# Strassen-form products for the first matmul of two MLPs, with operands streamed from DRAM and a planned instruction order

## Chip, cores and metric

The kernel runs on one core of one Trainium2 chip. The metric is device time in microseconds (us) of one execution; lower is better. The kernel before took 759.74 us (median of three runs, 759.37 to 760.29).

## What is computed

The input is q, k, v for 4 sequences of 576 tokens and 8 heads of 64. Attention is causal with a window of 128 and a linear bias by distance. Its output, 2304 tokens of 512 channels, goes through a first MLP (layer norm, 512 to 2048, relu, 2048 to 512, residual) and a second one (512 to 1024, relu, a gate made of a three-tap convolution along the sequence and a sigmoid, 1024 to 512):

```python
xn = (x - mu) / np.sqrt(var + 1e-06) * g_ln
x = x + np.maximum(xn @ w_ch1, 0.0) @ w_ch2
h = np.maximum(x @ w_in, 0.0)
conv_out += conv_w[k] * hp[:, k:k + S, :]          # k = 0, 1, 2
out = h * (1 / (1 + np.exp(-conv_out))) @ w_out
```

Weights arrive as 64-bit floats and are turned into 32-bit ones on the chip by integer operations on VectorE.

## The kernel before

The work is a pipeline on TensorE (PE) with three stages. Attention runs first (lines 333 to 737). The first MLP (lines 740 to 806) takes the 2304 tokens in six groups of 384 and, for each of 16 blocks of 128 hidden channels, calls `hidden` (line 314, first product) and `project` (line 759, second product). The second MLP (lines 809 to 963) takes the four sequences one by one: `hidden2` (line 869) makes one block of 128 hidden channels for 576 tokens, `gate_step` (line 884) runs relu, convolution, sigmoid and the split of the gated value, and `store` (line 819) makes the second product for 128 tokens and writes it out.

Every product is made three times: each operand is split into a high part (rounded, type fp32r, written by ScalarE) and a low part (the rest, written by VectorE), and high x high, high x low and low x high are summed in PSUM (`PASSES`, line 108). `split` (line 235) is the helper. So one block of `hidden` is 4 x 3 = 12 matmuls of 384 columns, one of `project` too, one of `hidden2` is 24 matmuls of 288 columns, and one `store` is 24 matmuls of 512 columns.

The order is written by hand. All engines issue in program order. In the first MLP, `hidden` of the next block stands ahead of `project` of the one before, so PE has 12 matmuls to do while ScalarE and VectorE split the hidden values. The layer norm of the next group is placed by tables of half steps (`LN_NEXT`, line 95), weight loads and conversions by `weights_step` (line 188), stores by `STORE_AT` (line 99). All weights of the first MLP stay in SBUF as high and low parts; those of the second are loaded in group 5 (lines 801 to 805) over them. Transfers are issued on SyncE's queue (SP).

Of the kernel before, what the change touches and what calls it, by code (L numbers as in the profile page):

```python
# [18 lines left out]
BIG = 2.0**110  # L19


@with_exitstack
def tile_kernel(
# [55 lines left out]
    NE = 7  # L79

# [9 lines left out]
    LN_SAME = {"spread2": {0: 1}}  # L90
    LN_FIRST = {
        "turn": {0: 6, 1: 9, 2: 11}, "root": {0: 13, 1: 14}, "gather": {0: 23}, "spread": {0: 25},
        "minus": {0: 27, 1: 28, 2: 29, 3: 30}, "parts": {0: 28, 1: 29, 2: 30, 3: 31},
    }
    LN_NEXT = {
        "turn": {0: 6, 1: 8, 2: 10}, "root": {0: 12, 1: 12}, "gather": {0: 14}, "spread": {0: 17},
        "minus": {0: 21, 1: 23, 2: 25, 3: 27}, "parts": {0: 22, 1: 24, 2: 26, 3: 28},
    }
    STORE_AT = {2: (0,), 3: ("mixed",), 4: (1,), 7: (2, 3)}
    SKIP = (4, 8, 12, 16, 20)  # L100
    LAST_CUTS = (256,)
    CONV_ACT = (0, 3, 5, 7)
    GATE_DVE = (0, 4, 6)
    VIA_PSUM = {"w1": 7, "w2": 9}
    SKIP_LAST = range(4, 31, 3)
# [9 lines left out]
    x = cpool.tile([P, NTT, DM], F32, tag="x", name="x")  # L115
    xT = x.rearrange("p t (c n) -> p t c n", n=P)

    pools = {"wearly": ctx.enter_context(tc.tile_pool(name="wearly", bufs=2 * NE))}
# [4 lines left out]
    c2pool.tile([P, 72], F32, tag="pad", name="pad")  # L123
# [5 lines left out]
    cvpool = xctx.enter_context(tc.tile_pool(name="cvpool", bufs=3, side="right"))  # L129
    dpool = xctx.enter_context(  # L130
        tc.tile_pool(name="dpool", bufs=2, space=bass.MemoryType.DRAM)
# [3 lines left out]
    fpool = xctx.enter_context(tc.tile_pool(name="fpool", bufs=2, side="right"))  # L135


    wtiles = {}
# [38 lines left out]
    def begin_loads(nm: str):  # L177
        scratch["raw"] = xnpool.tile([P, 3, 1024], I32, tag="xn_hl", name=f"raw_{nm}")
        scratch["n"] = 0
# [5 lines left out]
    COARSE = ((), ("rescale", 0, 1, 2), ("high", "low"))  # L185
    LAST = ((), ("rescale", 0, 1, 2), ("high",), ("low",))

    def weights_step(stages, start=True, only=None):
# [3 lines left out]
        for j in range(max((len(do) for _, do in now), default=0)):  # L192
            for ld, do in now:
                if j >= len(do):
                    continue
                kind, i, raw = ld["kind"], ld["i"], ld["raw"]
                if do[j] == "rescale":
                    t = ld["t"] = cvpool.tile([P, 512], I32, tag="cv", name=f"cv_{kind}_{i}")
                    if ld["via"]:
                        t = ld["mid"] = ps_x.tile([P, 512], I32, tag="px", name=f"cp_{kind}_{i}")  # L200
                    rescale(t, raw, G if stages is FINE else S)
                elif do[j] == "high":
                    w = wtiles[kind, i] = pools[ld["pool"]].tile(
                        [P, 2, 512], F32R, tag="w", name=f"{kind}_{i}"
                    )
                    S.activation(w[:, 0, :], ld["t"].bitcast(F32), AF.Copy)  # L206
                elif do[j] == "low":
                    w = wtiles[kind, i]
                    (G if stages is COARSE else V).tensor_tensor(  # L209
                        out=w[:, 1, :], in0=ld["t"].bitcast(F32), in1=w[:, 0, :].bitcast(F32),  # L210
                        op=ALU.subtract,
                    )
                    flight.remove(ld)
                else:
                    to_f32(ld["t"], raw, (do[j],), ld["mid"])
        if todo and start:
# [9 lines left out]
            else:  # L226
# [5 lines left out]
                "via": stages is COARSE and i >= VIA_PSUM[kind],  # L232
# [26 lines left out]
    def layer_norm(g: int, j: int, stage: str, pspool=None, tag=None):  # L259

        t = g * GT + j
        if stage == "turn":
            px = pspool.tile([P, NCC, P], F32, tag=tag, name=f"px_{t}")
            for c in range(NCC):
                T.transpose(px[:, c, :], xT[:, t, c, :], ident)
# [19 lines left out]
        elif stage == "gather":  # L285
# [5 lines left out]
            rows[g] = dpool.tile([2 * GT, P], F32, tag="rows", name=f"rows_{g}")  # L291
            nc.sync.dma_start(rows[g], mvt)
        elif stage in ("spread", "spread2"):

            i = stage == "spread2"
            b = bcs[g, i] = xnpool.tile([P, GT, P], F32, tag=f"bc{i:d}", name=f"bc{i:d}_{g}", bufs=1)
# [3 lines left out]
        elif stage == "minus":  # L300
            y = ys[g, j] = pools.get("y", fpool).tile([P, GT, P], F32, tag="y", name=f"xm_{g}_{j}")
            G.tensor_tensor(  # L302
                out=y, in0=xT[:, g * GT : (g + 1) * GT, j, :], in1=bcs[g, 0], op=ALU.subtract
            )
        else:
            if j == 0:
                xns[g] = xnpool.tile([P, 2, NCC, GN], F32R, tag="xn_hl", name=f"xn_hl_{g}")
# [6 lines left out]
    def hidden(g: int, f: int, pspool, tag: str):  # L314
        w = wtiles["w1", f]
# [9 lines left out]
        hh = hhs[g, f] = fpool.tile([P, 2, GN], F32R, tag="hh", name=f"hh_{g}_{f}")  # L325
# [7 lines left out]
    with ExitStack() as actx:  # L333
# [80 lines left out]
        reli = x[:, NTT - 3, 0:P].bitcast(I32)  # L414
# [11 lines left out]
        b0 = x[:, NTT - 4, 0:W]  # L426
        rows_i = x[:, NTT - 5, 0:NR].bitcast(I32)
        e = x[:, NTT - 5, 8 : 8 + NR]
        cb = x[:, NTT - 5, 16:20]
        sl = x[:, NTT - 5, 32 : 32 + NPAIR]  # L430
        ci = x[:, NTT - 6, 0:W].bitcast(I32)
        cf = x[:, NTT - 7, 0:W]
# [180 lines left out]
        def outputs(n: int):  # L613
# [3 lines left out]
            for u0, u1 in ((0, cut), (cut, 4)):  # L617
                if u0 < u1:
                    bl, pr, t = seq[n + u0]
                    t += bl * TPB  # L620
                    S.activation(xT[:, t : t + u1 - u0, pr, :], po[:, u0:u1], AF.Copy)
# [6 lines left out]
        for f in range(NF1):  # L628
            pool = "wearly" if f < NE else "wkeep" if f < NF2 else "wlate"
            todo += [("w1", f, pool), ("w2", f, pool)]  # L630
# [110 lines left out]
    pools["wkeep"] = ctx.enter_context(tc.tile_pool(name="wkeep", bufs=2 * NF2 - 2 * NE))  # L741
    ps_c = ctx.enter_context(tc.tile_pool(name="ps_c", bufs=1, space=PSUM, reuse_waits="tile"))
    with ExitStack() as fctx:
        pools["wlate"] = fctx.enter_context(tc.tile_pool(name="wlate", bufs=2 * (NF1 - NF2), reuse_waits="tile"))
        ps_h, ps_x = (
            fctx.enter_context(tc.tile_pool(name=n, bufs=2, space=PSUM, reuse_waits="tile"))
            for n in ("ps_h", "ps_x")
        )

        pcs = {}  # L750

        def residual(g: int, c: int, eng=G):
            xs = xT[:, g * GT : (g + 1) * GT, c, :]
            y = fpool.tile([P, GT, P], F32, tag="y", name=f"y_{g}_{c}")
            pc = pcs[g][c][:, :GN].rearrange("p (t n) -> p t n", n=P)
            V.tensor_tensor(out=y, in0=pc, in1=bcs[g, 1], op=ALU.mult)  # L756
            eng.tensor_tensor(out=xs, in0=y, in1=xs, op=ALU.add)  # L757

        def project(g: int, f: int):
            w, hh = wtiles["w2", f], hhs.pop((g, f))  # L760
            if f == 0:
                pcs[g] = [
                    ps_c.tile([P, 512], F32, tag=f"pc{c}", name=f"pc_{g}_{c}") for c in range(NCC)
                ]
            for c in range(NCC):
                pc = pcs[g][c]
                for n, (a, b) in enumerate(PASSES):
                    T.matmul(  # L768
                        pc[:, :GN], w[:, a, c * P : (c + 1) * P], hh[:, b, :],
                        start=f == 0 and n == 0, stop=f == NF1 - 1 and n == 2,  # L770
                    )
                if f == NF1 - 1 and g < NGRP - 1:
                    residual(g, c)

        steps = [(g, f) for g in range(NGRP) for f in range(NF1)]
        last = None
        for g, f in steps:
            for part in range(2):
                hs = 2 * f + part
                due = [(g, LN_SAME)]  # L780
                if g + 1 < NGRP:
                    due.append((g + 1, LN_NEXT if g else LN_FIRST))
                due = [
                    (gg, j, stage) for gg, table in due for stage, at in table.items()
                    for j in at if at[j] == hs
                ]
                for args in due:
                    if args[2] == "turn":
                        layer_norm(*args, ps_x, "px")
                if part == 0:  # L790
                    if (g, f) not in hhs:
                        hidden(g, f, ps_h, "ph")
                elif last is not None:
                    project(*last)
                for args in due:
                    if args[2] != "turn":
                        layer_norm(*args, ps_x, "px")
                if g == 0 or g == NGRP - 1:
                    weights_step(LAST if g else COARSE, 2 * f + part not in (SKIP if g == 0 else SKIP_LAST))
            last = (g, f)  # L800
            if g == NGRP - 1 and f == 0:
                begin_loads("win")
                for i in range(2 * NF2):
                    pool = "wearly" if i < 2 * NE else "wkeep"
                    todo.append(("win" if i < NF2 else "wout", i % NF2, pool))
        project(*last)


    bpool2, xpool = (
        ctx.enter_context(tc.tile_pool(name=n, bufs=b, reuse_waits="tile"))  # L810
        for n, b in (("bpool2", 2), ("xpool", 1))
    )
# [180 lines left out]
```

## Time and profile before

| what | us |
|---|---|
| runs: median (lowest to highest) | 759.74 (759.37 to 760.29) |
| profiled execution: span, first to last instruction | 757.7 |
| profiled execution: PE busy | 737.9 (97%) |
| PE weight load busy | 692.8 (91%) |
| VectorE (DVE) busy | 407.7 (54%) |
| ScalarE (ACT) busy | 314.7 (42%) |
| GpSimd (POOL) busy | 192.1 (25%) |

The profile gives the profiled execution's span, not its whole time; the median of the runs is 2.0 us above that span. To read it: one execution is shown; busy times are unions of the instructions of an engine. Matmuls are pipelined, so the mean of a single one (337 ns for 384 columns) is longer than the pitch at which they follow each other, and the pitch is read from chains of many. A share over the whole span mixes three stages with different limits.

### The profile page before, as it was taken

What the parts mean: (1) busy time and instruction counts of PE and PEld (TensorE: products, weight loads), DVE (VectorE), ACT (ScalarE), POOL (GpSimd) and SP (SyncE); (2) the same over time, 40 slices, a digit from 0 to 9 for tenths busy, and PEclk for the clock granted to TensorE, in tenths of its full rate; (3) what the DMA queues carried; (4) which work ended last, traced back from release to release, by engine and by line L of the source; (5) the groups of instructions that cost most, each with busy time, mean ns of one, the idle gap of its engine ahead of it and who ended that gap; (6) DMA issues with size and microseconds to landing.
All of it is one profiled execution on the core that took longest, in us unless ns stands there. A gap on an engine that the chain in (4) does not pass through costs nothing.

```text
span 757.7 us, 12569 instructions
## 1 busy us (share of the span) xinstructions
PE 737.9 (97%) x4896; PEld 692.8 (91%) x4896; DVE 407.7 (54%) x782; ACT 314.7 (42%) x840; POOL 192.1 (25%) x291
## 2 busy tenths in 40 slices
PE   7999998899999999999999999999999999999998
PEld 6777776799999999999999999999999889889987
DVE  6899999598732222122212312288789655456620
ACT  4888887545511111121112112154457554456521
POOL 1788789445620111112010221200023000000000
PEclk9999999999999999999999999999999999999999
DMA  6877765156300000000000000165100000000011
GB/s 149 186 188 164 190 164 133 33 187 176 113 12 8 4 1 11 11 1 10 1 12 1 12 12 1 25 208 179 44 1 1 28 15 29 29 28 15 15 42 56
DMA packets 81959, 47.25 MB, mean 62 GB/s; under 512 B 59440, under 2 KB 76652, under 8 KB 81900
## 3 DMA queue, kind: packets, MB, share of 16 engines
q1 hardware_dynamic: 80844, 46.20, 22.3%
q8 instruction: 38, 0.62, 0.4%
q10 hardware_dynamic: 1056, 0.26, 0.2%
q14 instruction: 21, 0.17, 0.1%
HBM read 41.71 MB, written 4.74 MB: 61 GB/s over the span
## 4 chain that ended last, share of the span: by engine, by line
PE 82%; DVE 11%; POOL 3%; ACT 2%; issue 1%; POOLq 0%; DVEq 0%; ACTq 0%
PE pc L768 25%; PE ph L320 25%; PE py L829 13%; PE pu L876 11%; PE ps L533 2%; DVE ps L544 2%; DVE pp L570 1%; PE po L608 1%; POOL pt L592 1%; DVE mn L548 1%; POOL pp L570 1%; DVE cv_w L172 1%; DVE cv_w L167 1%; PE ptp L580 1%; ACT pp L558 1%
## 5 line engine op out<-in xcount | busy, mean ns | idle before, releaser
L320 PE MATMUL ph<-xn_hl,w 128*128 128x384 f32 x1152 | 216.7, 337 | 0.0
L768 PE MATMUL pc<-hh,w 128*128 128x384 f32 x1152 | 215.7, 337 | 0.0
L768 PEld LDWEIGHTS pc<-hh,w 128*128 128x128 f32 x1152 | 200.6, 188 | 0.5 <-issue 0.2
L320 PEld LDWEIGHTS ph<-xn_hl,w 128*128 128x128 f32 x1152 | 200.2, 188 | 0.3 <-issue 0.2
L327 DVE SCALAR_TENSOR_TENSOR hh<-ph,hh 128x384 fp32r<-128x384 f32 x96 | 53.4, 556 | 205.8 <-ACT hh L326 205.6
L326 ACT ACTIVATE hh<-ph 128x384 fp32r<-128x384 f32 x96 | 47.1, 491 | 264.0 <-PE ph L320 263.9
L876 PEld LDWEIGHTS pu<-x,win 128*128 128x128 f32 x768 | 103.5, 188 | 1.6 <-ACT hp L889 0.6
L876 PE MATMUL pu<-x,win 128*128 128x288 f32 x768 | 104.5, 296 | 0.3 <-ACT hp L889 0.3
L829 PE MATMUL py<-wout,gm 128*128 128x512 f32 (+1 forms) x408 | 91.5, 382 | 0.0
L829 PEld LDWEIGHTS py<-wout,gm 128*128 128x128 f32 x408 | 73.0, 188 | 15.8
L902 DVE SCALAR_TENSOR_TENSOR cvo<-hp,cw,cvo 128x576 f32<-128x576 f32 x64 | 56.0, 875 | 3.7 <-POOL cvo L897 1.5
L558 ACT ACTIVATE pp<-ps,mn 128x128 f32<-128x128 f32 x144 | 51.3, 383 | 13.1 <-DVE mn L548 9.6
L302 POOL TENSOR_TENSOR xm<-x,bc 128x384 f32<-128x384 f32 x24 | 24.3, 1022 | 107.7 <-DVE xn_hl L244 57.9
L570 POOL TENSOR_SCALAR pp<-pp,sm 128x128 f32<-128x128 f32 x72 | 42.8, 604 | 33.1 <-DVE sm L567 30.5
L592 POOL TENSOR_SCALAR_AFFINE_SELECT pt<-pc 128x512 f32<-128x512 f32 x72 | 47.2, 684 | 1.7 <-ACT pc L585 1.4
L533 PE MATMUL ps<-kt,qt 64*128 64x256 f32 x288 | 44.0, 400 | 2.5 <-ACT pp L558 1.7
L608 PE MATMUL po<-pt,rawv 128*64 128x128 f32 x544 | 37.7, 280 | 7.8 <-POOL pt L592 5.6
L608 PEld LDWEIGHTS po<-pt,rawv 128*64 128x64 f32 x544 | 28.9, 136 | 16.2 <-POOL pt L592 13.3
L835 ACT ACTIVATE o<-py 128x512 f32<-128x512 f32 (+1 forms) x19 | 10.9, 575 | 64.3 <-PE py L829 64.3
L757 POOL TENSOR_TENSOR x<-y,x 128x384 f32<-128x384 f32 x20 | 19.6, 1015 | 66.3 <-DVE y L756 66.3
L239 DVE TENSOR_TENSOR gm<-cvo,gm 128x512 fp32r<-128x512 f32 x32 | 22.5, 703 | 23.7 <-ACT gm L238 23.6
L209 POOL TENSOR_TENSOR w<-cv_w,w 128x512 fp32r<-128x512 f32 x20 | 26.2, 1310 | 33.2 <-ACT w L206 31.9
(109 smaller groups left out, 812.3 us busy)
## 6 DMA issues: line engine op xcount, KB each, us to landing
raw_w<-in_moe_w_ch SPq DMA_DIRECT2D x32, 512.0 KB, 3.7
out<-o SPq DMA_DIRECT2D x17, 256.0 KB, 2.0
rawq<-in_q SPq DMA_DIRECT2D x32, 128.0 KB, 3.7
rawv<-in_v SPq DMA_DIRECT2D x32, 128.0 KB, 2.8
raw_win<-in_moe_w_in SPq DMA_DIRECT2D x8, 512.0 KB, 5.0
raw_win<-in_moe_w_out SPq DMA_DIRECT2D x8, 512.0 KB, 3.4
rawk<-in_k SPq DMA_DIRECT2D x30, 128.0 KB, 3.3
bc<-rows SPq DMA_DIRECT2D x12, 192.0 KB, 3.1
```

The lines of the kernel that those rows point to most:

```text
L320: T.matmul(ph[:, :GN], w[:, a, c * P : (c + 1) * P], xns[g][:, b, c, :], start=n == 0, stop=n == 3 * NCC - 1,)
L326: S.activation(hh[:, 0, :], ph[:, :GN], AF.Relu)
L327: V.scalar_tensor_tensor(out=hh[:, 1, :], in0=ph[:, :GN], scalar=0.0, in1=hh[:, 0, :].bitcast(F32), op0=ALU.max, op1=ALU.subtract,)
L533: T.matmul(ps[:, h, u, :].rearrange("p (o j) -> p o j", o=2), lhs, rhs, start=i == 0, stop=i == 1,)
L558: S.activation(pp[:, u, h, :], sc[:, h, u], AF.Exp, bias=mn[:, h, u : u + 1], scale=-1.0, accum_out=sm[:, 0, i : i + 1],)
L570: (G if i % 2 else V).tensor_scalar(out=pp[:, i, :], in0=pp[:, i, :], scalar1=sm[:, 1, i : i + 1], scalar2=1.0, op0=ALU.mult, op1=ALU.mult,)
L592: G.affine_select(out=parts[:, i], in_=pc, compare_op=ALU.is_ge, fill=0.0, base=base, pattern=[[0, 4], [sign, P]], channel_multiplier=-sign,)
L608: T.matmul(po[h * D : (h + 1) * D, u, :], rvs[bl, pr][:, t - 1 + i, h, :], pt[:, i, 2 * u + h, :], start=i == i0, stop=i == 1,)
L768: T.matmul(pc[:, :GN], w[:, a, c * P : (c + 1) * P], hh[:, b, :], start=f == 0 and n == 0, stop=f == NF1 - 1 and n == 2,)
L829: T.matmul(py[:, :w], lhs(a, f), wtiles["wout", f][:, b, c0:c1], start=n == 0, stop=n == 3 * NF2 - 1,)
L876: T.matmul(pu[:, i, :HS], w[:, a, c * P : (c + 1) * P], x2[:, i2, c, i * HS : (i + 1) * HS], start=n == 0, stop=n == 3 * NCC - 1,)
L902: V.scalar_tensor_tensor(out=cv, in0=hp[:, j : j + SEQ], scalar=cw[:, j * NF2 + f : j * NF2 + f + 1], in1=cv, op0=ALU.mult, op1=ALU.add,)
```

## The change

Only the two first products change arithmetically. Two blocks of tokens, two blocks of input channels and two blocks of hidden channels form 2 x 2 block matrices, whose product is made of 7 block products instead of 8, by sums of blocks of both operands. In the first MLP groups 0 and 1 stay as they were; groups (2, 3) and (4, 5) are the pairs, for 8 pairs of hidden blocks each (`superquad`). In the second MLP the two halves of each sequence are the pair, for 4 pairs of hidden blocks each (`quad2`). Each block product is 6 matmuls (2 channel blocks x 3 passes).

Operands. The seven token operands of a pair are made on chip (`x_operands`) and kept in SBUF over used weights. The seven weight operands of a pair of hidden blocks are made once, written to DRAM as split records of 128 x 512 (256 KB) and fetched again when needed: a transfer into one of three staging tiles, then a ScalarE copy that rounds it into one of 9 ring slots (`fetch`, `stream_record`). In the first pair of groups, hidden pairs 4 to 7 make four of the seven records on the spot from f32 weights fetched from DRAM. The weights of the second MLP are converted during the first (`prepare_wout`, `prepare_win`), go to DRAM, and come back later (`load_win`, `load_wout`).

Order. From the first MLP on every instruction is recorded in a `Plan` with an engine and a price in ns; PE's order is the program's, and the order on the other engines comes from a list schedule with due times taken from PE's order. Between the block products of a quad stand fillers: chunks of second products (12 / 2 = 6 matmuls) of the quad before, or of stores.

Other moves: x is stored by channel block, not by token tile; residual sums and layer-norm subtractions of the MLPs move from POOL to DVE; the hidden values of the second group of a pair are kept in f32 and rectified and split later (`second_half`).

```diff
+    def issue(self, rate=0.29, landing=1800, wait=200, rounds=6):
...
+    def products(out, items, start, stop):
...
+        ns = {384: 173, 288: 134, 512: 232, 256: 118}[n]
...
+    XB21, XB11, XT2, XT1, XT3, XT4, XB22 = range(7)
+    PRODUCT = {
+        1: (WA11, XB11), 2: (WA12, XB21), 3: (WS4, XB22), 4: (WA22, XT4),
+        5: (WS1, XT1), 6: (WS2, XT2), 7: (WS3, XT3),
+    }
...
+    def x_operands(put, b11, b12, b21, b22):
+        put(XB21, b21)
+        put(XB11, b11)
+        tt(b12, b22, b12, ALU.subtract)
+        tt(b11, b12, b11, ALU.add)
+        put(XT2, b11)
+        put(XT3, b12)
+        tt(b12, b22, b11, ALU.subtract)
+        put(XT1, b12)
+        tt(b21, b21, b11, ALU.subtract)
+        put(XT4, b21)
+        put(XB22, b22)
...
+    NSTAGE = 3
...
+    def fetch(dst, src, key=None, stage=None, eng="S"):
...
+        plan.add("SP", 70, lambda: nc.sync.dma_start(stage(), src), [src], [key], nbytes=262144)
+        if eng == "S":
+            plan.add("S", 590, lambda: S.activation(dst, stage(), AF.Copy), [key], [dst])
...
+    def stream_record():
...
+        t = slot_at(n % NRING)
+        if s == 2 or p < PEARLY or j in (WA11, WA12, WA22):
+            fetch(t, w1d[p][j])
+            return
+        if j == WS2:
...
+                dma(cv, w1f[2 * p + i], 262144)
...
+        parts_of(u[:, 0, :], u[:, 1, :], sb if j in (WS2, WS4) else sa)
+        dma(w1d[p][j], t.bitcast(F32), 262144)
...
+    QUAD = ("P2", "P1", "F", "F", "P6", "P5", "P7", "F", "F", "P4", "P3")
+    def quad(n: int, take, done, xop, steps, after):
+        out = {1: Z, 6: Z, 7: Z, 4: Z, 5: E, 3: E, 2: BB}
...
+    def superquad(s: int, p: int, extra):
...
+            if st == "P1":
+                act(sn[0], Z[:, :GN])
+                tt(tmp, BB[:, :GN], sn[0], ALU.add)
+            elif st == "P6":
+                act(sn[1], Z[:, :GN])
+            elif st == "P7":
+                act(sn[0], Z[:, :GN])
+                add_h(f1, sn[0], E)
+            elif st == "P4":
+                rect_parts(hhr[:, 1, 0, :], hhr[:, 1, 1, :], Z[:, :GN])
+            elif st == "P3":
+                add_h(f0, sn[1], E)
...
+    for s in (1, 2):
...
+        for p in range(NF1 // 2):
+            if s == 1:
+                extra.append(lambda p=p: prepare_wout(p))
+            elif p % 2 == 0:
+                extra.append(lambda p=p: prepare_win(p // 2))
...
+            superquad(s, p, extra)
+        fillers(len(fill))
+        for c in range(NCC):
+            residual(2 * s, c)
+        if s == 1:
+            for fn in second_half(3):
+                fn()
...
+    NHP = 6
+    hp_ring = [fav(i * HPW, SEQ + 2) for i in range(NHP)]
...
+    LEAD = 14
+    halves = second_half(5)
+    load_win(0)
+    load_win(1)
+    prepare_x2(0)
+    for fn in halves[:LEAD]:
+        fn()
+    load_win(2)
+    load_win(3)
+    fill += halves[LEAD:]
...
     for b in range(B):
+        for p in range(NF2 // 2):
+            if (b, p) == (1, 0):
+                load_wout(range(NF2 - 1))
...
+            if b and (b, p) != (1, 0) and len(fill) < 4 and jobs:
+                fill += store_chunks(*jobs.pop(0))
+            quad2(b, p, QUAD)
+        if b + 1 < B:
+            prepare_x2(b + 1)
+    fillers(len(fill))
+    for job in jobs:
...
+    plan.issue()
```

## Rows read from the trace of the kernel before

**Rows 1.** Page: busy time by engine, and the 40 slices of PE and its clock.

```profile
PE 737.9 (97%) x4896; PEld 692.8 (91%) x4896; DVE 407.7 (54%) x782; ACT 314.7 (42%) x840; POOL 192.1 (25%) x291
...
PE   7999998899999999999999999999999999999998
...
PEclk9999999999999999999999999999999999999999
```

**Rows 2.** Windows: us; PE, PEld, DVE, ACT, POOL busy (count); clock, DMA share, GB/s.

```profile
20.00:40.00 20.00, 19.85 (x214) 16.30 (x215) 16.61 (x41) 17.24 (x74) 14.78 (x26) 1.00 0.87 196
...
100.00:120.00 20.00, 16.90 (x185) 13.36 (x182) 19.12 (x43) 15.23 (x64) 17.05 (x25) 1.00 0.63 153
500.00:520.00 20.00, 20.00 (x117) 20.00 (x116) 17.96 (x33) 9.91 (x18) 0.13 (x2) 1.00 0.60 184
...
570.00:590.00 20.00, 19.65 (x134) 18.51 (x133) 19.05 (x32) 15.16 (x33) 5.45 (x4) 1.00 0.00 1
590.00:715.00 125.00, 125.00 (x753) 113.61 (x752) 71.25 (x121) 66.10 (x132) 0.00 (x0) 1.00 0.06 24
```

**Rows 3.** The chain that ended last, in order of time: start us, us, what.

```profile
205.54 2.08 PE ph L320 x12
207.62 2.08 PE pc L768 x12
...
582.28 0.55 ACT hp L889
582.83 0.04 issue
582.87 3.46 PE pu L876 x24
...
693.64 6.40 PE pu L876 x48
700.04 5.61 PE py L829 x24
...
715.25 39.39 PE py L829 x192
```

**Rows 4.** Groups of PE by form: count, busy us, mean ns, idle before.

```profile
L320 PE MATMUL ph<-xn_hl,w 128*128 128x384 f32 x1152 | 216.7, 337 | 0.0
...
L876 PE MATMUL pu<-x,win 128*128 128x288 f32 x768 | 104.5, 296 | 0.3 <-ACT hp L889 0.3
```

**Rows 5.** Timeline in the first MLP: start us, us, engine, line, instruction.

```profile
301.74 1.55 PE L768 MATMUL pc<-hh,w 128*128 128x384 f32 x8
301.94 0.49 ACT L326 ACTIVATE hh<-ph 128x384 fp32r<-128x384 f32 x1 [4.11 <-PE ph L320]
```

**Rows 6.** Groups of ACT by form: count, busy us, mean ns, idle before.

```profile
L326 ACT ACTIVATE hh<-ph 128x384 fp32r<-128x384 f32 x96 | 47.1, 491 | 264.0 <-PE ph L320 263.9
...
L206 ACT ACTIVATE win<-cv_win 128x512 fp32r<-128x512 f32 x8 | 5.1, 632 | 7.5 <-DVE cv_win L172 7.5
...
L835 ACT ACTIVATE o<-py 128x256 f32<-128x256 f32 x2 | 0.8, 384 | 4.8 <-PE py L829 4.8
```

**Rows 7.** Groups of DVE by form: count, busy us, mean ns, idle before.

```profile
L902 DVE SCALAR_TENSOR_TENSOR cvo<-hp,cw,cvo 128x576 f32<-128x576 f32 x64 | 56.0, 875 | 3.7 <-POOL cvo L897 1.5 <-ACT cvo L895 1.0
L327 DVE SCALAR_TENSOR_TENSOR hh<-ph,hh 128x384 fp32r<-128x384 f32 x96 | 53.4, 556 | 205.8 <-ACT hh L326 205.6
...
L909 DVE TENSOR_TENSOR cvo<-cvo,hp 128x576 f32<-128x576 f32 x27 | 20.3, 752 | 0.0
...
L756 DVE TENSOR_TENSOR y<-pc,bc 128x384 f32<-128x384 f32 x24 | 12.8, 553 | 5.4 <-POOL x L757 5.4
...
L239 DVE TENSOR_TENSOR gx<-cvo,gx 128x64 fp32r<-128x64 f32 x32 | 8.1, 254 | 32.2 <-ACT gx L238 32.2
```

**Rows 8.** Page: DMA packets, and DMA issues with KB each and us to landing.

```profile
DMA packets 81959, 47.25 MB, mean 62 GB/s; under 512 B 59440, under 2 KB 76652, under 8 KB 81900
...
out<-o SPq DMA_DIRECT2D x17, 256.0 KB, 2.0
rawq<-in_q SPq DMA_DIRECT2D x32, 128.0 KB, 3.7
...
raw_win<-in_moe_w_in SPq DMA_DIRECT2D x8, 512.0 KB, 5.0
raw_win<-in_moe_w_out SPq DMA_DIRECT2D x8, 512.0 KB, 3.4
```

More of the change, by code (lines that the diff above doesn't have):

```diff
@@ L947, in tile_kernel @@
[L947 to L963 removed]
+    r2pool = ctx.enter_context(tc.tile_pool(name="r2pool", bufs=1))
@@ new lines, in tile_kernel @@
+    r2 = late["r2"] = r2pool.tile([P, 2 * (NF1 - NE) * WT], F32R, tag="r2", name="r2")
+    psm = ctx.enter_context(tc.tile_pool(name="psm", bufs=1, space=PSUM, reuse_waits="tile"))
+    bank = [psm.tile([P, 512], F32, tag=f"bank{i}", name=f"bank{i}") for i in range(8)]
+    plan = Plan()
+    for t in (x, r1, r2, hhr, xn, fa, cw, gain):
+        plan.know(t, "sb")
+    for t in bank:
+        plan.know(t, "bank")
+    small = xnpool.tile([P, 48], F32, tag="small", name="small", bufs=1)
+    mvt2 = xnpool.tile([2 * GT, P], F32, tag="mvt2", name="mvt2", bufs=1)
@@ new lines, in project @@
+    def project(f: int, cs, first: bool, last: bool):
+        w = wtile("w2", f)
+        hh = hhr[:, f % 2]
+        for c in cs:
+            products(
+                bank[c][:, :GN], [(w[:, a, c * P : (c + 1) * P], hh[:, b, :]) for a, b in PASSES],
+                first, last,
+            )
+    FKEEP = 8
+    PEARLY = 4
+    w1f = [dram(f"w1f{f}", [P, 512], F32) for f in range(NF1)]
+    w1d = [[dram(f"w1d{p}_{j}", [P, 512], F32) for j in range(7)] for p in range(NF1 // 2)]
+    wind = [[dram(f"wind{p}_{j}", [P, 512], F32) for j in range(7)] for p in range(NF2 // 2)]
@@ new lines, in tile_kernel @@
+    Z, E, BB, PX = (bank[4 + i] for i in range(4))
+    QUAD = ("P2", "P1", "F", "F", "P6", "P5", "P7", "F", "F", "P4", "P3")
+    assert [PRODUCT[int(s[1])][0] for s in QUAD if s != "F"] == list(W_ORDER)
+    def quad(n: int, take, done, xop, steps, after):
+        out = {1: Z, 6: Z, 7: Z, 4: Z, 5: E, 3: E, 2: BB}
+        first, final = {1, 5, 2}, {4, 3, 2}
+        for i, st in enumerate(steps):
+            if st[0] == "P":
+                m = int(st[1])
+                j, k = PRODUCT[m]
+                w, xo = take(j), xop(k)
+                products(
+                    out[m][:, :n],
+                    [(w[:, a, h, :], xo[:, b, h, :]) for h in range(2) for a, b in PASSES],
+                    m in first, m in final,
+                )
+                done()
+            else:
+                st = st if st != "F" else None
+            after(i, st)
```

1057 lines of the change are left out of this document (804 added, 253 removed).

## Prediction

> **What bounds the kernel now.** I read the page first: PE is busy 97% of the span at granted clock 1.00, no other engine over 54% [rows 1]. The windows show where that holds: in attention other engines run close to full beside it (DVE 19.12 of 20 us, PE 16.90), and from about 140 us on PE is without a gap except 0.35 us near 583 us [rows 2]. The chain of waits says the same for the two MLPs: blocks of 12 matmuls of 384 columns follow each other every 2.08 us (173.3 ns each), 24 of 288 columns take 3.20 us (133.3 ns each; 6.40 for 48), 24 of 512 columns 5.61 us [rows 3]. ACT idles 263.9 us behind the hidden block alone [rows 6]. So in the MLPs the time is the number of matmuls times their pitch, and what other engines do is free as long as PE doesn't wait for it. Attention keeps its instructions; I take it as unchanged.
>
> **What is removed.** A superquad (two groups, two hidden blocks) needed 8 x 6 = 48 matmuls of 384 columns and gets 42: 6 x 173.3 = 1.04 us, times 2 pairs x 8 = 16: 16.6 us. A quad of the second MLP loses 6 of 48 with 288 columns: 0.80 us, times 16: 12.8 us. Counts check: 1152 becomes 1056 and 768 becomes 672 [rows 4]. The second products keep theirs; the pitch per form has no reason to change, each matmul still brings its own weight load. **Gross gain: 29.4 us**, which only comes if PE stays gapless. The rest is what the new dependences take back.
>
> **PSUM evacuation: -2.2 and -3.0.** Bank Z now takes four products in turn with a reading by ACT between them. The hop is visible: the next PE block starts at 301.74, ACT starts on the finished bank at 301.94, so 0.20 us, then 0.49 us of copy [rows 5]; from ACT's end to PE's next matmul 0.04 us [rows 3]. Together 0.73 us. Between P1 and P6 and between P7 and P4 two fillers (2.08 us) cover it; the last (P4 to the next P1) has P3 and P2. But P6 to P7 has only P5: 6 x 173.3 = 1.04 us against 0.73. In the second MLP it is 0.80 against 0.20 + about 0.41 (288 columns, between 384 ns for 256 and 491 for 384 [rows 6]) + 0.04 = 0.65. What lies in the way is a 632 ns copy of a fetched record that ACT has just begun; ACT's load is near 75%, so lateness is between 0 and 0.63 us each, 0 to 20 us for 32. The schedule knows ACT's durations nearly right (it prices this copy 590), so I take a sixth of the upper end: 0.1 each, 3 us. Three evacuations have no filler because the list is empty or nearly so (P7 to P4 in the first superquad of the first pair, both gaps in that of the second): 3 x 0.73 = 2.2 us.
>
> **Handover of the accumulators: -1.0.** After each pair the fillers are flushed, `residual` reads four banks on DVE (two operations of 0.553 us each per bank [rows 7]) and `second_half` wants the first bank again after three bank-blocks of 0.52 us. Four banks need 8 x 0.553 + 0.2 = 4.6 us if strictly in turn, PE wants the last after about 3.1: between 0 and 1.5 us, twice; taken 0.5 each.
>
> **DVE in the second MLP: -4.0.** New per quad: three additions of 288 columns, about 0.46 us (between 254 ns for 64 and 553 for 384 columns [rows 7]); gates as before, 4 x 0.875 + 2 x 0.752; so 6.4 us, and 0.43 per store chunk in place of the split before: 8.1 us a quad against 5.60 + 4 x 1.40 = 11.2 us of PE. Making token operands for the next sequence is 11 operations of 576 columns, 8.3 us. By sequence, DVE against PE: first 38 against 39 (fillers there are 18 chunks left of `second_half`), second 44 against 41 (its first quad has two fillers and the last residual), third 41 against 45. So DVE is asked for 98% of some 125 us, where it had 57% (71.25 of 125 [rows 2]). What eases it: gates aren't needed by PE until the sequence's stores begin, and six buffers let them lag three quads. The trace has a comparable stretch: 570 to 590, DVE at 19.05 of 20 and PE losing 0.35 [rows 2]. If DVE lost 8% more to hops, 10 us, most would be lag. Between 0 and 10; taken 4, about 1 per change of sequence and 1 at the entry.
>
> **Traffic: -2.5.** 108 records are written and 148 fetched, 256 KB each: 67 MB on top of 47.25 [rows 8]. ACT's 140 extra copies, 140 x 0.632 = 88 us, lie in the 264 us that it idles. In the second pair a superquad is 66 matmuls, 11.44 us of PE, and moves 7 fetches + 3.5 stores + 512 KB raw, about 3.3 MB, 286 GB/s. The first pair's later half needs 9 records, 2 stores and 512 KB raw: 3.4 MB, 298 GB/s. The most the trace moves in 20 us is 196 GB/s, but at DMA share 0.87 with short packets; large weight loads made 184 at share 0.60, 307 at full share [rows 2]. So it fits narrowly. The other limit is three staging tiles: each is held from the issue until ACT has copied it. At 2.0 us to landing, that of a 256 KB store [rows 8], plus 0.4 for ACT to come free and 0.63: 3.0 us per cycle, 7 records in 7 us. It breaks even at 11.44 x 3 / 7 = 4.9 us, a landing of 3.9. Behind a store on SP that waits for DVE's low part stand the next fetches; nine ring slots are 14 us of cover. Between 0 and 32 us (landing 5.0, the row of the 512 KB weight load, makes the cycle 6.03 us, which costs 2.6 us in each of the 12 superquads with all seven fetched); I take 2.5, nearest the landing of its own size.
>
> **At nothing:** operands of a pair (8 x 0.553 + 11 x about 0.95 = 15 us of DVE, 768 columns extrapolated from 384 and 576) lie beside group 1's 66 us and the 33 us of `second_half`; DVE there has also sums for four hidden pairs, some 19 us. If that cover fails, it costs at most the missing part of 15 us, once or twice. Weight conversion has the same three operations per load. Residuals move from POOL to DVE, 24 x 0.55 us, beside PE. The last 7 stores stay as they are, 39.39 us [rows 3].
>
> **Sum.** -29.4 + 2.2 + 1.0 + 3.0 + 4.0 + 2.5 = -16.7 us. Against the profiled execution, 757.7 us of span and some 2.0 around it (the median of the runs stands there), that is **743.0 us**.
>
> **Rivals.** (1) The schedule hides nearly all; only handovers and uncovered evacuations remain, 3.2, and 1 to 2 more: 735. For it: the 0.35 us beside a 95% DVE. Against: each new margin is 0.1 to 0.3 us. (2) DVE and ACT together become the bound from the entry of the second MLP on: all 10 us there and 6 for P6 to P7 in place of 7: 752. For it: 98%; against: lag is allowed. (3) **Slower:** the fetch loop decides in the superquads. In-order ACT stands at a copy whose record hasn't landed, the evacuation of Z stands behind it, PE waits. From a landing of 3.9 us it costs, 28 us per us of landing (12 x 7 / 3); at 4.6 it has eaten 16.7 + 2.5, at 5.0 it gives 743 - 2.5 + 32 = 772. For it: 3.7 for 128 KB under load, 5.0 for 512 KB [rows 8]; against: both are with packets of 256 B or 1 KB, and 3.4 with 4 KB ones. (4) Transfers don't overlap: 9 to 11 records a superquad (fetches and stores), one by one at 2.0 us, are 18 to 22 us, some 9 over the 11.44 in each of 16: about 890. Against it: 196 GB/s with transfers of 128 KB that take 3.7 us each means five in flight [rows 2, 8]. [...] (5) The gain is there and lost exactly, no effect: 760.
>
> **Chances.** The sum as forecast (738 to 749) 0.48, (1) 0.15, (2) 0.13, (3) 0.17, (4) 0.02, (5) 0.05. A measurement of this kernel tells 0.2%, 1.5 us. Faster: forecast, (1) and (2), 0.76; same: nearly (5), 0.04; slower 0.20. The range reaches from (1)'s better half to (3)'s first half: 733 to 766.
>
> **What would show it.** Right: 1056 and 672 first-product matmuls at 173 and 133 ns; two or three PE gaps of 0.7 us at the start of a pair; gaps of 0.1 to 0.3 us ahead of P7; DVE over 90% in the second MLP with PE still over 95%; 114 MB moved; landings of fetches under 3.5 us. Wrong: PE gaps of a microsecond in every superquad behind ACT and a DMA (3), PE under 95% behind DVE in the second MLP (2), a lower granted clock or a longer pitch of the 384-column matmuls, or attention itself longer.

## The result, and the profile after

The changed kernel took 747.05 us (median of four runs, 745.31 to 748.11) against 759.68 for the one before: a ratio of 0.9826, interval 0.9805 to 0.9846, so 13 us faster, where 16.7 were forecast (743.0, range 733 to 766). The profiled execution is the 745.31 one, the fastest of the four, with a span of 743.6 us, 14.1 less than before.

The page, busy time by engine and the slices of PE, DVE and the clock, answers to [rows 1]:

```profile
PE 716.6 (96%) x4704; PEld 667.4 (90%) x4704; DVE 536.8 (72%) x1073; ACT 476.1 (64%) x1190; POOL 145.8 (20%) x248
...
PE   8999998899899999999999999999999999999998
...
DVE  5799999569999836555678665558468999687631
...
PEclk9999999999999999999999999999999999999999
```

PE has 192 matmuls fewer (4896 to 4704), twice 96 as counted, and is still the busiest engine; DVE and ACT each work some 130 to 160 us more. The windows answer to [rows 2], with the same columns:

```profile
180.00:200.00 20.00, 18.34 (x109) 17.66 (x107) 19.37 (x32) 10.18 (x19) 10.48 (x12) 1.00 0.73 217
200.00:220.00 20.00, 19.62 (x104) 19.08 (x105) 18.17 (x24) 8.38 (x16) 8.95 (x7) 0.91 0.55 173
300.00:320.00 20.00, 20.00 (x117) 19.98 (x116) 10.67 (x22) 12.04 (x25) 0.00 (x0) 1.00 0.92 306
...
440.00:460.00 20.00, 20.00 (x117) 20.00 (x117) 11.27 (x24) 13.39 (x28) 0.00 (x0) 1.00 0.84 279
560.00:580.00 20.00, 18.86 (x126) 18.18 (x125) 18.05 (x32) 18.44 (x38) 0.00 (x0) 1.00 0.48 141
580.00:600.00 20.00, 18.81 (x106) 16.09 (x105) 18.89 (x36) 17.80 (x42) 0.00 (x0) 1.00 0.16 53
620.00:640.00 20.00, 20.00 (x120) 18.05 (x119) 16.79 (x34) 14.51 (x32) 0.00 (x0) 1.00 0.07 27
```

The superquads (300 to 320 and 440 to 460 us) are full, with DMA shares of 0.84 to 0.92. What is lost lies elsewhere: in group 0 (180 to 220 us), a stage that the change was to leave alone, and at the change of sequence in the second MLP (560 to 600). The chain of waits, answering to [rows 3], is one block of PE over six superquads, and over most of the end; its first row here is four transpositions (start us, us, what):

```profile
241.82 0.44 PE bank L1031 x4
...
297.05 70.20 PE bank L989 x402
...
424.79 85.65 PE bank L989 x489
...
587.64 152.93 PE bank L989 x867
```

The list of waits on PE names what the gaps are (who waited for whom: us in total, times, longest). L989 is the matmul of every product, L952 any ScalarE copy or activation, L959 any VectorE addition or subtraction, L1062 the transposition of the layer norm's roots, and L1057 the last operation that makes them:

```profile
PE bank L989 <- ACT fa L952: 4.3, 5, 1.3
PE bank L1062 <- POOL small L1057: 3.0, 3, 2.0
PE bank L989 <- DVE fa L959: 1.9, 3, 0.9
```

To put a figure on each place I take PE's start-to-start times in the trace, less the pitch of the form (173.5, 133.3, 233.7 ns, within 0.2 of [rows 3]; 110 ns for a transposition, from the row of four above). This counts the whole gap, also what a modelled end of a matmul hides; below it is called "by the pitch". From the first block of the first MLP on this sums to 6.4 us in the kernel before and 19.9 in the changed one. By stretch the difference is +5.2 in groups 0 and 1 (to 292 us), +5.3 in the two pairs (to 515), +4.1 to 600 us, -1.1 after. The 39 transpositions for the norms of groups 3 to 5, which the change moves into group 1 from later groups, are work and not counted as loss. With 1.8 us that attention took longer in this execution, -29.4 + 13.5 + 1.8 = -14.1: the whole change of the span. By the medians of the runs the gain is 1.5 us smaller; no trace shows where these went.

### The profile page after: what moved, and what is told of

Its sections match the earlier page's. It is cut to its first block, busy times and chain, and to the rows that moved or that the text cites. A ratio compares the mean times of both kernels' runs of the same rounds, so it can differ in the third digit from the quotient of the medians.

```text
span 743.6 us, 13429 instructions
## 1 busy us (share of the span) xinstructions
PE 716.6 (96%) x4704; PEld 667.4 (90%) x4704; DVE 536.8 (72%) x1073; ACT 476.1 (64%) x1190; POOL 145.8 (20%) x248
## 2 busy tenths in 40 slices
DMA packets 122303, 114.63 MB, mean 154 GB/s; under 512 B 63552, under 2 KB 87292, under 8 KB 122236
## 4 chain that ended last, share of the span: by engine, by line
PE 63%; DVE 3%; DMA 2%; ACT 2%; POOL 1%; issue 1%; SPq 0%; ACTq 0%; POOLq 0%; DVEq 0%
PE bank L989 63%; DVE fa L959 1%; DMA w1d<-r 1%; ACT fa L952 1%; DMA fa<-in_moe_w_out 1%; ACT r L1258 0%; PE bank L1031 0%; DMA h<-woutd 0%; DVE small L1039 0%; POOL small L1053 0%; DVE hhr L967 0%; DVE x L959 0%; DVE xn L967 0%; DVE xn L959 0%; DVE fa L353 0%
## 5 line engine op out<-in xcount | busy, mean ns | idle before, releaser
L989 PE MATMUL bank<-hhr,r 128*128 128x384 f32 x1152 | 214.5, 338 | 1.1 <-DVE fa L959 1.0
L989 PE MATMUL bank<-r,r 128*128 128x288 f32 (+1 forms) x1248 | 204.7, 315 | 5.2 <-ACT fa L952 4.3
L989 PEld LDWEIGHTS bank<-r,r 128*128 128x128 f32 x1248 | 193.8, 188 | 9.4 <-ACT fa L952 6.1
L989 PEld LDWEIGHTS bank<-hhr,r 128*128 128x128 f32 x1152 | 199.3, 188 | 2.3 <-DVE fa L959 1.7
L1258 ACT ACTIVATE r<-fa 128x512 fp32r<-128x512 f32 x115 | 70.6, 626 | 23.2 <-DMA fa<-w1d 9.7
L989 PE MATMUL bank<-r 128*128 128x512 f32 (+2 forms) x360 | 81.2, 370 | 0.3 <-ACT r L1258 0.3
L952 ACT ACTIVATE fa<-bank 128x288 f32<-128x288 f32 (+1 forms) x112 | 49.5, 442 | 38.1 <-PE bank L989 36.2
L989 PEld LDWEIGHTS bank<-r 128*128 128x128 f32 x360 | 64.0, 188 | 10.0 <-ACT r L1258 0.7
L989 PE MATMUL bank<-xn,r 128*128 128x384 f32 x360 | 68.5, 339 | 0.1
L989 PEld LDWEIGHTS bank<-xn,r 128*128 128x128 f32 x360 | 63.8, 191 | 0.4 <-POOL r L1157 0.4
L959 DVE TENSOR_TENSOR fa<-bank,fa 128x288 f32<-128x288 f32 (+1 forms) x88 | 43.6, 500 | 28.2 <-ACT fa L952 17.6
L952 ACT ACTIVATE hhr<-bank 128x384 fp32r<-128x384 f32 x46 | 22.5, 490 | 56.4 <-PE bank L989 56.0
L952 ACT ACTIVATE r<-fa 128x256 fp32r<-128x256 f32 (+2 forms) x94 | 47.6, 519 | 14.4 <-DVE fa L353 10.1
L967 DVE SCALAR_TENSOR_TENSOR fa<-fa,cw 128x576 f32<-128x576 f32 x64 | 51.1, 812 | 1.3 <-ACT fa L952 0.8
L959 DVE TENSOR_TENSOR r<-fa,r 128x256 fp32r<-128x256 f32 (+1 forms) x74 | 37.7, 521 | 11.6 <-ACT r L952 9.0
L989 PE MATMUL bank<-r,hhr 128*128 128x512 f32 (+1 forms) x192 | 44.5, 381 | 0.0
```

The lines of the kernel that those rows point to most:

```text
L952: "S", 160 + 0.84 * cols(out), lambda: S.activation(out, src, func, **kw),
L959: "V", 40 + 1.3 * cols(out), lambda: V.tensor_tensor(out=out, in0=a, in1=b, op=op),
L967: lambda: V.scalar_tensor_tensor(out=out, in0=a, scalar=sc, in1=b, op0=op0, op1=op1),
L989: T.matmul(out, lhs, rhs, start=start and n == 0, stop=stop and n == len(items) - 1, skip_group_check=True,)
L1258: plan.add("S", 590, lambda: S.activation(dst, stage(), AF.Copy), [key], [dst])
```

## The experiments

All are the changed kernel with one edit or a few. Ratios are to the kernel before on the same chip; a difference to the changed kernel is the difference of the ratios times 759.7 us, and by the intervals of the two ratios it is known to 2 or 3 us.

**Put the eighth product back.** P2 is made twice:

```diff
+                if m == 2:
+                    products(out[m][:, :n], [...], True, True)
```

> The first of the seven products, P2, is made twice in every quad (the second time over the first, in the same bank), so that the first products have as many matmuls as in the kernel before, 8 for 8, and everything else of the change stays. Theory A (PE is the limit in nearly every quad, so the seven-for-eight saving is real at 29.4 us and the rest of the change costs some 16 us against it): 29.4 us slower than the changed kernel, less at most 3 us where the extra product covers a wait: 773.5 to 776.5, that is slower than the kernel before by 14 to 17 us. Theory B (in the quads ScalarE, VectorE or the transfers are so close to the limit that PE's time isn't what counts): under 25 us slower, below 772.

773.22 us, ratio 1.0166 (1.0143 to 1.0189): 26 us slower than the changed kernel, of 29.4 for 192 matmuls. (By the spans of the profiles it is 28.7, 772.3 against 743.6, but the one is the slowest of its four runs and the other the fastest.) That is just under Theory A's range and above Theory B's 25 us: the seven-for-eight saving is real almost in full, and all that comes with it costs 13 us by itself.

**Take the cover from one evacuation.**

```diff
-    QUAD = ("P2", "P1", "F", "F", "P6", "P5", "P7", "F", "F", "P4", "P3")
+    QUAD = ("P2", "P1", "F", "F", "F", "P6", "P5", "P7", "P4", "F", "P3")
```

> One filler is moved from between P7 and P4 to before P6 and the other to after P4, so that P4 follows P7 at once in every quad and waits for ScalarE's reading of bank Z without cover; no work is added. Theory A (0.20 + 0.49 + 0.04 us per uncovered evacuation, about 0.1 more as seen at the three places of the changed kernel where it is uncovered, 0.75 to 0.9 us; 0.65 to 0.75 in the second MLP): 15 x 0.8 + 16 x 0.7 = 23 us slower, about 770, and P6 to P7 behind P5 alone still shows no wait. Theory B (PE's order has slack elsewhere that takes it up): under 10 us slower.

787.61 us, ratio 1.0376 (1.0334 to 1.0419), 42 us slower, not 23. This order changes part of the computation: the filler behind P4 multiplies hidden values that P4 has just replaced, and so it waits for them too. The timeline of PE over one superquad shows both:

```profile
324.73 1.03 PE L989 MATMUL bank<-r,r 128*128 128x384 f32 x5
326.40 1.31 PE L989 MATMUL bank<-r,r 128*128 128x384 f32 x6 [0.64 <-ACT fa L952]
328.29 0.44 PE L989 MATMUL bank<-hhr,r 128*128 128x384 f32 x1 [0.58 <-ACT hhr L952]
328.89 1.15 PE L989 MATMUL bank<-hhr,r 128*128 128x384 f32 x5 [0.15 <-DVE hhr L967]
329.87 1.22 PE L989 MATMUL bank<-r,r 128*128 128x384 f32 x6
```

P4 (the second row) starts about 0.9 us late by the pitch in each superquad and 0.77 in the second MLP's quads: some 26 us more than in the changed kernel, as Theory A says. The filler's 0.58 + 0.15 (1.3 by the pitch) in 14 superquads make most of the rest. P6 behind its fillers, P5 and P7 follow without a gap: the 1.04 us of P5 are enough.

**Two staging tiles.** `NSTAGE = 2` for 3.

> Two staging tiles instead of three for the fetched records. In the changed kernel a fetch of w1d takes 3.9 us to landing (median), which with 0.4 and 0.63 us for the copy makes a cycle of 4.9 us, and three tiles carry seven records in 11.44 us: just the break-even of the prediction, and no superquad waits. Theory A (the 3.9 us are mostly queueing behind other transfers issued early, and shrink when fewer are in flight): landing falls toward 2.5 us, seven records take 3.5 x 3.5 = 12.4 us at most, and the kernel is 0 to 15 us slower than 747. Theory B (3.9 us is what a transfer takes beside this traffic): seven records take 17.2 us, 5.7 more than PE's 11.44 in 12 superquads with seven fetches: some 65 us slower, about 812.

756.42 us, ratio 0.9951 (0.9931 to 0.9971): 9.5 us slower. The rows of the fetch, first of the changed kernel, then of this one, and PE's wait in this one:

```profile
fa<-w1d SPq DMA_DIRECT2D x96, 256.0 KB, 3.9
```

```profile
fa<-w1d SPq DMA_DIRECT2D x96, 256.0 KB, 3.0
```

```profile
PE bank L989 <- ACT r L1258: 7.5, 9, 1.9
```

Landing falls from 3.9 to 3.0 us with two tiles, when fewer fetches are in flight, so Theory A: at least 0.9 of the 3.9 us are other transfers in flight. PE now waits for fetched copies, 9 times (10 us by the pitch), all between 468 and 510 us, in the second pair, where every superquad fetches seven records; the first four superquads of the first pair fetch seven too and do not wait. So the third tile buys the second pair. The forecast's sum for the loop is too strict: two tiles at a landing of 3.0 give 14.1 us for seven records against 11.44, some 32 us over 12 superquads, and 9.5 were lost; and in the changed kernel the median from 296 to 510 us is 4.2, above the break-even of 3.9, without a wait.

**Fillers for the first superquad of each pair.** The last four chunks of the group before are held back:

```diff
-            for fn in second_half(3):
+            half3 = second_half(3)
+            for fn in half3[:-4]:
                 fn()
+            fill += half3[-4:]
```

(and blocks 14 and 15 of group 1 alike).

> At the start of each pair of groups four chunks of second products are held back as fillers for the first superquad (blocks 14 and 15 of group 1; the last four chunks of group 3), where the changed kernel has none or too few. Theory A (the three gaps of 0.9 us at 296, 420 and 424 us are evacuations of bank Z without cover): all three go, 2.5 us faster, about 744.5. Theory B (they are late operands, since the token operands of the pair are made just before): the gaps stay, or come at the first product, P2; no gain.

747.26 us, ratio 0.9826 (0.9809 to 0.9842): no gain. The gaps at 296, 420 and 424 us are gone, as Theory A says, but by the pitch two of 0.6 and 0.7 us are at 440 and 308, and one of 4.3 us has come at 446, with 6.8 us at the lower granted clock behind it (2.9 us more). ACT's timeline there:

```profile
443.34 0.42 ACT L952 ACTIVATE r<-fa 128x256 fp32r<-128x256 f32 x1
449.00 0.66 ACT L333 ACTIVATE fa<-fa 128x512 f32<-128x512 f32 x1 [5.24 <-DMA fa<-in_moe_w_in]
449.56 0.48 ACT L952 ACTIVATE hhr<-bank 128x384 fp32r<-128x384 f32 x1
```

A transfer of raw weights, issued at 440.81, was still out; ACT stood in front of its conversion, and the evacuation of bank Z stood behind it in ACT's queue. This is the forecast's rival (3), once.

**The roots earlier.** The reciprocal roots are recorded one hidden block ahead of the transposition that reads them:

```diff
                 if f == f0 + GT:
+                    norm_root(gg)
+                if f == f0 + GT + 1:
                     norm_gather(gg, bank[7])
```

> The reciprocal roots of groups 1 to 5 are recorded one hidden block earlier on POOL than the transposition on PE that reads them; nothing else is edited. Theory A (in the changed kernel PE stands still at these five transpositions, 0.19 to 2.12 us each, 3.9 us in all, because POOL's six small operations are issued right in front of them): the five waits fall below 0.1 us each and the kernel is 3.5 to 5.5 us faster than the changed kernel, so 741.5 to 743.5; if the stretch at the lower granted clock from 201.6 us on follows from the 2.12 us wait, it goes too (1.6 of the 5.5). Theory B (PE would only wait elsewhere, since VectorE runs at 18 to 19 of 20 us around the 198 us mark): the waits move to the next blocks and the time stays within 1 us of 747. Theory C: the stretch at the lower clock is independent of the wait and stays.

744.52 us, ratio 0.9786 (0.9765 to 0.9807), 3 us faster, between the two theories. Four of the five waits are gone, as in Theory A; that near 200 us stays (2.5 us by the pitch), and two of 1.5 and 1.2 us on DVE's and POOL's results have come, as in Theory B. The lower clock followed the remaining wait again (mean granted clock of this execution 0.998).

**The table load earlier.** A sigmoid of one column at the start of the first MLP.

> One more ScalarE instruction, a sigmoid of one column, is recorded at the start of the first MLP, so that the table load of 1.28 us that stands at 541.4 us in the changed kernel comes hundreds of us earlier. Theory A (the 1.58 us that PE loses at 542 us is the table load in front of the evacuation of bank Z): that gap goes, the kernel is 1.3 to 1.6 us faster, so about 745.5. Theory B (ScalarE is overloaded there anyway, with 14 copies of fetched weights in the 25 us around): half of the gap stays or comes back within the next two quads, gain under 0.5 us.

745.48 us, ratio 0.9811 (0.9788 to 0.9833). The gap at 542 us is gone from the trace and nothing comes in its place there; the time alone (1 us) doesn't tell. In the changed kernel ACT's timeline had:

```profile
541.36 1.28 ACT L952 ACT_TABLE_LOAD   x1
542.65 0.68 ACT L952 ACTIVATE fa<-fa 128x576 f32<-128x576 f32 x1
543.24 0.39 ACT L952 ACTIVATE fa<-bank 128x288 f32<-128x288 f32 x1
```

The last row is the evacuation that PE waited for. The plan prices a sigmoid as any other activation and doesn't know of the load.

**Copies of w_out on POOL.** `fetch(..., eng="G")` in `load_wout`.

> The 16 copies of the fetched w_out records, 0.63 us each on ScalarE, are put on POOL, which is idle there. Theory A (between 566 and 589 us ScalarE, busy 18.1 of 20 us, is what PE waits for: gaps of 1.40, 1.13 and 0.69 us): the three gaps shrink to under 0.5 us in all, gain 2.7 to 3.2 us, about 744. Theory B (VectorE, 18.5 of 20 us there, is the limit, as the prediction had it): the gaps stay within 1 us of what they are. Theory C (POOL's copies slow VectorE, as its operations beside POOL's were slower in the kernel before, 649 against 556 ns): slower by 1 to 4 us.

752.56 us, ratio 0.9899 (0.988 to 0.9918): 5.5 us slower: Theory C's direction, beyond its 4 us. By the pitch PE's waits from 574 to 599 us are 7.5 us instead of 3.2, and 3.4 us at the lower granted clock follow the longest of 2.8. Groups of DVE from 560 to 600 us, the changed kernel first; the second of each has one input in PSUM:

```profile
L959 DVE TENSOR_TENSOR r<-x,r 128x576 fp32r<-128x576 f32 x7 | 5.2, 754 | 0.6 <-ACT r L952 0.6
L959 DVE TENSOR_TENSOR fa<-bank,fa 128x288 f32<-128x288 f32 x11 | 5.0, 453 | 0.7 <-ACT fa L952 0.5 <-PE bank L989 0.2
```

```profile
L959 DVE TENSOR_TENSOR r<-x,r 128x576 fp32r<-128x576 f32 x7 | 6.6, 952 | 0.2 <-ACT r L952 0.2
L959 DVE TENSOR_TENSOR fa<-bank,fa 128x288 f32<-128x288 f32 x10 | 4.5, 451 | 2.1 <-PE bank L989 1.1 <-ACT fa L952 1.0
```

Beside POOL's copies (15 of 752 ns in these 40 us, where POOL had nothing in the changed kernel) the operation with both inputs in SBUF went from 754 to 952 ns, and the addition with one input in PSUM kept its time, 453 and 451 ns. What makes the difference between the two was not shown.

**No copies of w_out at all.**

```diff
-                fetch(t, woutd[f][h], *next_stage(OUT_STAGE))
+                next_stage(OUT_STAGE)
```

> The changed kernel without the 16 fetches and ScalarE copies of the w_out records: the second products of the second MLP use what lies in that memory, all else is computed as before. It is the test that the copies on POOL could not be, since those slowed VectorE. Theory A (ScalarE, 18.1 of 20 us busy from 560 to 600 us, holds PE up there): the waits of 1.40, 1.13 and 0.69 us at 574, 582 and 587 us go, 2.5 to 3.2 us faster, 744. Theory B (VectorE, 18.5 of 20 us, holds it up): the waits stay within 1 us of what they are.

745.34 us, ratio 0.9798 (0.9765 to 0.983), 2 us faster, no more than the intervals allow. By the pitch the waits of 1.40, 1.13 and 0.69 us became 0.76, 1.87 and none: those behind ACT shrank by 1.3 us in all, that behind DVE grew by 0.7. So most of it moved rather than went, closer to Theory B. Both engines are nearly full there (in the changed kernel DVE 18.05 and 18.89 us of each 20 from 560 us on, ACT 18.44 and 17.80), and relief on ACT handed part of the wait to DVE.

**Norms of group 2 moved to group 1,** with the roots and the table load early.

> Three edits of the order together: the statistics of group 2 are recorded in group 1 instead of group 0 (where VectorE converts weights and is busy 19.4 of 20 us), the roots one block earlier than the transposition that reads them, and the early sigmoid for the table load. Theory A (the wait of 2.1 us near 198 us comes from VectorE's backlog of conversions in group 0, in front of the roots, and the 3.4 us at the lower granted clock that follow it come from that wait): no wait over 0.3 us between 150 and 290 us, no stretch at the lower clock there; 3.9 + 1.6 + 1.5 = 7 us faster than the changed kernel, 740. Theory B (VectorE's backlog just reaches PE elsewhere in group 0, as in the run where only the roots were moved, with new waits of 1.4 and 1.1 us): 2 to 3 us faster, 744 to 745.

746.0 us, ratio 0.9822 (0.9797 to 0.9847): no gain, so Theory B's mechanism without its 2 to 3 us. The wait on the roots is gone and PE waits for weights instead, behind POOL's low parts and ACT's high parts of w1 and w2:

```profile
PE bank L989 <- POOL r L1162: 1.8, 2, 0.9
...
PE bank L989 <- ACT r L952: 1.1, 2, 0.9
```

So with the statistics out of the way the conversions are late. Their three steps, among DVE's groups from 150 to 224 us in the changed kernel:

```profile
L348 DVE SCALAR_TENSOR_TENSOR fa<-fa 128x512 int32<-128x512 int32 x10 | 10.9, 1092 | 0.2
L353 DVE SCALAR_TENSOR_TENSOR fa<-fa 128x512 int32<-128x512 int32 x10 | 9.5, 948 | 0.2
...
L343 DVE TENSOR_SCALAR bank<-bank 128x512 int32<-128x512 int32 x10 | 6.9, 688 | 0.3 <-ACT bank L333 0.3
L348 DVE SCALAR_TENSOR_TENSOR bank<-fa,bank 128x512 int32<-128x512 int32 x10 | 6.8, 684 | 0.0
L353 DVE SCALAR_TENSOR_TENSOR fa<-fa,bank 128x512 int32<-128x512 int32 x10 | 6.8, 680 | 0.4
L343 DVE TENSOR_SCALAR fa<-fa 128x512 int32<-128x512 int32 x10 | 5.8, 584 | 3.7 <-ACT fa L333 3.7
```

Every second conversion works over SBUF, beside POOL's 1.3 us subtractions, and takes 0.57 us longer than one over a PSUM bank (584 + 1092 + 948 against 688 + 684 + 680 ns). The mean hides two sorts: of the 20 steps at L348 and L353 over SBUF, 13 took 0.68 to 0.70 us and seven 1.3 to 1.8, and each of the seven has POOL at work beside it for 0.8 us or more; the 20 over PSUM took 0.65 to 0.70 us, eleven of them beside POOL. The kernel before had 16 of these 20 conversions over PSUM (line 104).

**All conversions over PSUM.** `bank[6 + n % 2]` for every one, on top of the last.

> As the run with the norms moved (746.0), and every weight conversion in group 0 works over a PSUM bank, not every second one: in the changed kernel the three integer steps take 688, 684 and 680 ns over PSUM but 584, 1092 and 948 ns over SBUF, beside POOL's subtractions; the kernel before had 16 of these 20 over PSUM. Theory A (VectorE's backlog of 10 x 0.57 = 5.7 us in group 0, brought by the choice of SBUF for every second conversion, is what the waits of 5 to 7 us between 164 and 291 us come from): they fall below 2 us, the kernel is 3 to 5 us faster than with the norms moved alone, 741 to 743. Theory B (the bank that conversions share, or the transfers of raw weights, take the place): within 1.5 us of 746.

757.2 us, ratio 0.9962 (0.9946 to 0.9978): 10 us slower, in neither theory's range, and yet it tells most. The wait list:

```profile
PE bank L1031 <- DVE fa L353: 13.2, 2, 12.6
```

The first statistics of group 1 write bank 7, and six blocks' conversions recorded ahead of them now hold it: the bank of Theory B. The wait is 12.9 us by the pitch, and 13.7 us at the lower granted clock follow. But once that is over, PE has no gap above 0.2 us from 185 to 244 us.

**The same with another bank for the statistics.**

```diff
-                    norm_turn(gg, f - f0, bank[7])
+                    norm_turn(gg, f - f0, bank[4 + (f + 1) % 2])
...
-                    norm_gather(gg, bank[7])
+                    norm_gather(gg, bank[4 + (f + 1) % 2])
```

> As the run with all conversions over PSUM, but the transpositions for the statistics write the bank that the hidden block of the next turn uses, not the one that conversions recorded six blocks ahead have taken (there PE stood 12.8 us at 150 us and 13.7 us at the lower clock followed; from 185 to 244 us it didn't wait at all). Theory A (VectorE's backlog of conversions over SBUF is the cause of the waits in groups 0 and 1, and the shared bank alone spoiled the last test): the 12.8 us go, waits between 150 and 291 us are 1.5 us at most in all against 6 in the changed kernel (7.5 with the norms moved), and the time is 738.5 to 742. Theory B (hidden blocks and statistics now wait for each other's bank): new waits at the transpositions of 0.5 us or more each, 12 of them, time above 744.

743.91 us, ratio 0.9782 (0.9758 to 0.9807): 3.3 us faster than the changed kernel and 3.0 than with the norms moved, but outside Theory A's range and short of Theory B's: waits of 5 us remain before 291 us (three of 1.0 to 1.6 us behind DVE and POOL near 200 us, and three, not 12, of 0.6 at transpositions, which stood in the two runs before as well). The backlog is smaller, not gone.

**And with held fillers.**

> The run before with four fillers held back at the start of each pair of groups as well. Theory A (the wait of 4.3 us at 446 us in the first run with held fillers was one late transfer of raw weights, landing 8 us after its issue, in front of an evacuation on ScalarE, by the chance of that order): 2.5 us faster than the run before, 736 to 739.5. Theory B (the held fillers push the fetches of the second pair together, so that such a wait comes again): one or two waits of over 1.5 us between 425 and 500 us, and no gain.

741.95 us, ratio 0.9753 (0.9727 to 0.9778), the fastest kernel here: 18.8 us under the one before. It is outside Theory A's range, and Theory B's waits are there in part: two of 1.3 us at 441 and 472 us, none of 4. The run before is 2 us slower, but the two intervals overlap, so that the held fillers gain some of their 2.5 us is likely, not shown.

## Why the prediction was right, and where it was off

- **Gross gain, 29.4 us:** right. The counts are as given, the pitch holds (70.20 us for 402 matmuls is 174.6 ns), and the eighth product, put back, costs 26 us.
- **Evacuations, 2.2 + 3.0:** the three uncovered ones came where they were said, 0.91 + 0.85 + 0.91 = 2.7 us. The 3.0 us for P6 to P7 were not there: the traces show no gap at it, and 1.04 and 0.80 us of P5 cover 0.73 and 0.65.
- **Handover, 1.0:** 0.86 + 0.73 = 1.6 us, at 385 and 513.
- **DVE in the second MLP, 4.0:** 3.2 us between 574 and 587, plus 1.6 for a table load that the forecast didn't have. The size is near, the mechanism half right: DVE worked 105.8 us of the 125 from 545 on (85%, not 98), and only 1.13 of the 3.2 us are a wait for it. 1.40 are an uncovered evacuation, P7 to P4 in the second sequence's first quad, whose list of fillers is empty (the forecast's count of three left it out), and 0.69 a copy of a w_out record on ACT. Lag was allowed, as argued, and after 600 us PE waits no more.
- **Traffic, 2.5:** nothing in the changed kernel. Landing was 3.9 us, the break-even of the forecast, not under 3.5, and yet no superquad waited; the run with held fillers met rival (3) once, and that with two tiles nine times. 114.63 MB moved, 114 forecast.
- **The term that failed** is "At nothing: ... Weight conversion has the same three operations per load", with the layer norms beside it. Groups 0 and 1 lost 5.2 us that the sum had at 0. In the changed kernel's trace they are five waits, 3.9 us, for roots issued right before the transposition that reads them, and 1.6 us lost at half the clock (0.50 granted from 202 to 205 us) behind the longest of them. Behind these stand conversions over SBUF that take 2.62 instead of 2.05 us, with DVE at 19.37 of 20: they are what PE waits for once the roots are moved. I had counted operations by kind and not by where their operands lie, nor read how far the recorded order puts a producer ahead of its reader.
- Terms missed (5.2 + 1.6) and terms not spent (3.0 + 2.5) nearly cancel, which is why the total was close: the gross gain was understood, the sum of the costs came out by luck. That attention took 1.8 us more in this execution goes in part with two stretches at the lower clock in it (3.4 us each at 0.50, from 13.9 and 119.7 us): of six other profiles of the changed stages without such a stretch there, five start the first MLP 0.1 to 0.7 us earlier than the kernel before, but one 1.4 us later.

The prediction's first paragraph also misread the stage. It has PE without a gap from about 140 us on, but the windows of the kernel before show 1.1 and 0.8 us lost there, with DVE at 18.32 of 20 already:

```profile
140.00:160.00 20.00, 18.89 (x150) 18.18 (x145) 12.29 (x19) 8.57 (x16) 8.13 (x9) 1.00 0.30 89
160.00:180.00 20.00, 19.16 (x114) 18.84 (x113) 18.32 (x30) 10.16 (x20) 9.49 (x12) 1.00 0.56 175
```

Open: what holds the three waits near 200 us in the last two kernels wasn't tried further. DVE is at 19.22 of 20 in the last, and the layer-norm subtractions that the change moved to it, both inputs in SBUF, took 1115 ns there against 548 in the first run with all conversions over PSUM. Why the clock falls in attention in some executions only (0.98 up to 143 us in the changed kernel, 1.00 up to 141 in the one before) is open too.

## What to carry to other kernels

The saving of multiplications on a nearly gapless PE was worth almost its count times its pitch here (26 of 29.4 us), and can be checked by putting one product back. The costs sat not in the new inner loop, which was planned to the tenth of a us, but at its seams and in the stage ahead of it: read how far each producer is issued ahead of its reader, and price an operation by where its operands lie and what runs beside it (the same integer step took 0.65 to 0.70 us over PSUM and up to 1.8 over SBUF beside POOL). ACT works its queue in order (with held fillers it stood 5.24 us in front of one conversion, an evacuation behind it): keep copies that wait for transfers away from evacuations, or give them a buffer more than the mean asks for (the third tile was worth 9.5 us).

## What the runs showed of the hardware that was not expected

- PE's granted clock fell to half (0.50 in the trace) behind most of its long waits: 2.1 us at 198 us in the changed kernel (0.91 over the next window, above), 2.8 at 586 in the run with copies on POOL, 4.3 at 446 with held fillers, 12.9 at 150 with all conversions over PSUM. It did not fall after 2.4 us at 196 in the run with held fillers, nor after 2.2 us at 490 with two staging tiles, and without the cover it fell at 458 us after waits of 0.9 us and less. At half the clock matmuls of 384 columns follow each other every 0.32 us instead of 0.1735; the stretch of 3.4 us after the wait at 198 us cost 1.6.
- Such stretches come in attention too, in some profiles and not in others of the same stages: two of 3.4 us in the changed kernel's, none in that of the kernel before.
- Integer steps of DVE with two inputs (L348, L353) and all operands in SBUF took 0.68 to 0.70 us where POOL worked beside them for 0.6 us or less, and 1.3 to 1.8 where it did for 0.8 us or more; over PSUM they took 0.65 to 0.70 either way.
- A load of ACT's function table, at 541.36 us, took 1.28 us and stalled PE by 1.58 where it stood in front of an evacuation of PSUM.
